# A float32 attention and two-layer expert chain: layers 1 and 3 as 2x2 block products with seven multiplications

## The chip, the core and the metric

The kernel runs on one core of a Trainium2 chip. Its five engines each work through a queue of their own in order: TensorE (PE, with its weight loads PEld), VectorE (DVE), ScalarE (ACT), GpSimd (POOL) and SyncE (SP, which issues most transfers). They wait for each other through semaphores. The metric is the device time of one execution in microseconds (us), lower is better; the median of three runs is given.

## The reference

A clustered attention gives 1536 tokens of 512 values, and four dense products follow:

```python
x = attention(q, k, v, centroids)            # (1536, 512)
h = max(max(x @ w1, x @ w2), x @ w3)         # layer 1: three weights 512 x 768
y = h @ w_out                                # layer 2: 768 x 512
g = max(y @ w_in, 0) ** 2                    # layer 3: 512 x 2048
out = g @ w_out2                             # layer 4: 2048 x 512
```

Weights come from HBM as 64-bit floats.

## The kernel before

Each float32 operand is held as a high and a low part in the fp32r type; a product of two operands is three matmuls (high x high, high x low, low x high). A matmul takes a 128 x 128 weight block and a chunk of 512 tokens, of which there are three, into one of eight PSUM banks. The attention part is ordered by a planner with costs and due times and is not touched, save that four constant tiles move to a pool of their own (`ac`) which ends with the attention. The text below speaks of what follows it.

Layer 1 takes its weights one at a time: 6 row blocks `fi` times 3 matrices `j`, each 512 columns wide in SBUF. `products` (L236 to L241) issues 36 matmuls per weight (4 k blocks x 3 parts x 3 chunks). The banks come in two sets `psu` of three. ACT copies the result of j = 0 to `hm` (L907), DVE takes the maximum for j = 1 and 2 (L909), and ACT and DVE split the maximum into `h` (L910, L911). Layer 2 does 4 x 54 matmuls in the same way, split into `yT` (L922, L923). Layer 3 has 16 row blocks `fi` of 36 matmuls; relu, square and split (L964 to L969) make `g`. Layer 4 (`mm_out`, L939) adds two `fi` at a time into 12 token tiles: six matmuls into a bank of their own, then DVE adds the bank to the sum `acc` in SBUF (L949). Its matmuls stand between those of layer 3.

A weight block of 512 columns is loaded as raw bits (`w_load`, L189) into one of three `wr` tiles and turned into float32 by six DVE instructions (`w_bits`, L208 to L214) and a POOL addition (L215); `w_parts` makes the high part on ACT (L227) and the low part on POOL (L228). Two weights (`EARLY`) are converted during the attention, so that the last stretch of it also holds first matmuls of layer 1. What belongs to the next weights is issued by `ahead` after the matmuls of this one; the program's order is written out by hand.

Of the kernel before, what the change touches and what calls it, by code (L numbers as in the profile page):

```python
# [2 lines left out]

# [80 lines left out]
BIG = float(2.0 ** 100)  # L84


@with_exitstack
def clustered_attention_moe(ctx, tc, qT, kT, vv, cen, w123, wo1, win, wo2, out):
    nc = tc.nc
# [79 lines left out]
    use = list(range(U2)) + [u_in(fi) for fi in range(NF)]
    plan = [[u] for u in use[EARLY:]] + [[]] * (EARLY + 1)  # L170
    for fi in range(NF):
        s = FIRST[fi] if fi < len(FIRST) else U2 + fi
        plan[s] = plan[s] + [u_out(fi)]
    seq = use[:EARLY] + sum(plan, [])
    assert sorted(seq) == list(range(len(units)))
# [42 lines left out]
    def w_parts(i):  # L218
        _, n = units[i]
        if i < EARLY:  # L220
            hl = wearly.tile([P, 2, 512], F32R, tag="whl", name=f"whl{i}")
        elif i >= U2 and (i - U2) % 4 >= 2:
            hl = wl.tile([P, 2, 512], F32R, tag="w2", bufs=6, name=f"w2_{i}")
        else:
            hl = wl.tile([P, 2, 512], F32R, tag="whl", bufs=3, name=f"whl{i}")
        t = wval.pop(i)
        act.copy(hl[:, 0, :n], t)  # L227
        pool.tensor_tensor(hl[:, 1, :n], t, f(hl[:, 0, :n]), op=ALU.subtract)  # L228
        wspl[i] = hl
# [652 lines left out]

    def blocks(u, *sb):

        yield ps2[u], [t[:, :1024].rearrange("p (a b) -> p a b", a=2) for t in sb]
        yield ps1[u], [t[:, 1024:] for t in sb]

    with ExitStack() as hctx:
        hp_ = hctx.enter_context(tc.tile_pool(name="hp_", bufs=1, reuse_waits="tile"))
        hsb = hp_.tile([P, FF1 // P, 2, NTOK], F32R, name="h")  # L890
        for fi in range(FF1 // P):
            hm = hp_.tile([P, NTOK], F32, tag="hm", bufs=2, name=f"hm{fi}")
            for j in range(3):
                w = next_w()
                u = (3 * fi + j) % 2
                pt = psu[u]
                if fi == 0 and j < EARLY:
                    products(pt, w, HP - 1, xT, HP - 1, False, True, (1,))
                    for k in range(HP):
                        products(pt, w, k, xT, k, k == 0, k == HP - 1, (2,))  # L900
                else:
                    for k in range(HP):
                        products(pt, w, k, xT, k, k == 0, k == HP - 1)
                ahead()
                for ps, (sb,) in blocks(u, hm):
                    if j == 0:
                        act.copy(sb, ps)  # L907
                    else:
                        dve.tensor_tensor(sb, ps, sb, op=ALU.max)  # L909
            act.copy(hsb[:, fi, 0, :], hm)  # L910
            dve.tensor_tensor(hsb[:, fi, 1, :], hm, f(hsb[:, fi, 0, :]), op=ALU.subtract)  # L911
        yT = xp.tile([P, DM // P, 2, NTOK], F32R, tag="xy", name="yT")
        for m in range(DM // P):
            pt = psu[m % 2]
            for kk in range(2):
                w = next_w()
                for k3 in range(3):
                    k = kk * 3 + k3
                    products(pt, w, k3, hsb, k, k == 0, k == FF1 // P - 1)
                ahead()  # L920
            for ps, (hi, lo) in blocks(m % 2, yT[:, m, 0, :], yT[:, m, 1, :]):
                act.copy(hi, ps)  # L922
                dve.tensor_tensor(lo, ps, f(hi), op=ALU.subtract)  # L923

    gp = ctx.enter_context(tc.tile_pool(name="gp", bufs=1, reuse_waits="tile"))
    NTT = NTOK // P
    GF = 2
    NG = FF2 // P // GF
    HALF = NTT // GF
    acc = [gp.tile([P, DM], F32, name=f"acc{t}") for t in range(NTT)]  # L930
    gs = {}

    def mm_out(gi, tk, n=slice(0, DM), pt=None):
        fs = range(gi * GF, gi * GF + GF)
        pt = pso[tk % 2] if pt is None else pt
        c = slice(tk * P, tk * P + P)
        for fi in fs:
            for a, wi in ((0, 0), (0, 1), (1, 0)):
                pe.matmul(pt[:, n], gs[fi][:, a, c], wspl[u_out(fi)][:, wi, n], start=fi == fs[0] and a + wi == 0,  # L939
                          stop=fi == fs[-1] and a == 1)  # L940
        return pt

    def out_add(gi, tk, pt, n=slice(0, DM)):
        if gi == 0 and tk < 2:
            act.copy(acc[tk], pt)
        elif gi == 0:
            dve.tensor_copy(acc[tk], pt)
        else:
            dve.tensor_tensor(acc[tk][:, n], pt[:, n], acc[tk][:, n], op=ALU.add)  # L949
        if gi == NG - 1:  # L950
            sp.dma_start(out[tk * P : tk * P + P, n], acc[tk][:, n])

    for fi in range(FF2 // P):
        w = next_w()
        pt = psu[fi % 2]
        for k in range(HP):
            products(pt, w, k, yT, k, k == 0, k == HP - 1)
        ahead()
        rt = gp.tile([P, NTOK], F32, tag="rt", bufs=1, name=f"rt{fi}")
        gt = gp.tile([P, 2, NTOK], F32R, tag="g", bufs=2 * GF, name=f"g{fi}")  # L960
        h0, h1 = slice(0, S), slice(S, 2 * S)
        todo = []
        for ps, (sb,) in blocks(fi % 2, rt):
            act.activation(sb, ps, AF.Relu)  # L964
        for h in (h0, h1):
            todo.append(lambda h=h, fi=fi: ((pool if fi >= 2 and h == h0 else dve).tensor_tensor(rt[:, h], rt[:, h], rt[:, h], op=ALU.mult),
                                     act.copy(gt[:, 0, h], rt[:, h])))  # L967
        for h in (h0, h1):
            todo.append(lambda h=h, fi=fi: (pool).tensor_tensor(gt[:, 1, h], rt[:, h], f(gt[:, 0, h]), op=ALU.subtract))  # L969
        gi = fi // GF - 1  # L970
        for i in range(HALF):
            if gi >= 0:
                tk = fi % GF * HALF + i
                out_add(gi, tk, mm_out(gi, tk))

            if todo and (fi != GF or i):
                todo.pop(0)()
        gs[fi] = gt
    for tk in range(NTT - 1):
        out_add(NG - 1, tk, mm_out(NG - 1, tk))  # L980

    for i in range(2):
        n = slice(i * DM // 2, (i + 1) * DM // 2)
        pt = ps1[i]
        out_add(NG - 1, NTT - 1, mm_out(NG - 1, NTT - 1, n, pt), n)
# [42 lines left out]
```

## Time and profile before

| | us |
|---|---|
| three runs | 717.44, 717.85, 717.99 (median 717.85) |
| profiled execution, first to last instruction (span) | 716.1 |
| median less that span | 1.75 |
| attention, with the first matmuls of layer 1 | 0 to 264.43 |
| rest of the two early weights (30 matmuls) | 264.43 to 271.23 |
| layer 1 | 271.23 to about 402 |
| layer 2 | about 402 to 451 |
| layers 3 and 4 | about 451 to 713.0 |
| last addition and store | 713.0 to 716.1 |

The page of the profile gives the busy time of each engine and a chain of work that ended last; a matmul's own time overlaps that of the next, so a busy PE is judged by how many matmuls a stretch holds.

### The profile page before, as it was taken

The page shows a single profiled execution, that of the slowest core. Times are in us where ns is not written, and L with a number is a line of the kernel's source. Part 1 is how long each engine was busy: PE and PEld are TensorE (multiplying, and loading weights), DVE is VectorE, ACT ScalarE, POOL GpSimd, SP SyncE. Part 2 cuts the span into 40 slices and gives each one's busy share as a digit, 9 for nine tenths or more (in the row PEclk, how much of TensorE's full clock was granted, in tenths as well). Part 3 has the DMA queues.
Part 4 walks back from the last instruction along what each step waited for, and adds up shares of the span by engine and source line. Part 5 has one row for each costly group of instructions (what it writes and reads, how often), then busy time and mean ns, then how long its engine had stood idle before and what let it go on. Part 6 is the DMA issues. An engine that isn't in the chain of part 4 may idle for free.

```text
span 716.1 us, 10433 instructions
## 1 busy us (share of the span) xinstructions
PE 701.3 (98%) x3663; PEld 597.1 (83%) x3663; DVE 588.4 (82%) x915; ACT 336.3 (47%) x670; POOL 449.0 (63%) x386
## 2 busy tenths in 40 slices
PE   7799999999999999999999999999999999999998
PEld 6689898999999878888888888888888888888886
DVE  6788988989989988998897677798888888886434
ACT  5789999999999841122212121333222222223210
POOL 5477797796867865553663233477776667777530
PEclk9999999999999999999999999999999999999999
DMA  8973834615432002221322032111111111210004
GB/s 215 240 179 91 203 89 130 154 43 136 106 109 89 1 30 88 89 88 59 118 74 67 25 101 84 63 59 60 59 59 59 59 59 64 89 54 1 1 0 177
DMA packets 21108, 62.21 MB, mean 87 GB/s; under 512 B 3168, under 2 KB 3936, under 8 KB 20608
## 3 DMA queue, kind: packets, MB, share of 16 engines
q1 hardware_dynamic: 20336, 59.98, 28.8%
q10 hardware_dynamic: 720, 1.57, 0.7%
q8 instruction: 29, 0.48, 0.3%
q14 instruction: 23, 0.19, 0.1%
HBM read 38.83 MB, written 3.15 MB: 59 GB/s over the span
## 4 chain that ended last, share of the span: by engine, by line
PE 88%; DVE 7%; ACT 2%; issue 2%; POOL 1%; DMA 0%; ACTq 0%; DVEq 0%; POOLq 0%
PE psd L240 29%; PE pss L939 18%; PE pss L240 15%; PE pss L572 6%; PE psd L533 4%; PE pss L592 4%; PE psd L535 4%; PE pss L593 4%; DVE at L583 2%; DVE nm L542 2%; PE pss L423 2%; ACT at L578 1%; ACT e L549 1%; PE pss L132 1%; PE pss L449 1%
## 5 line engine op out<-in xcount | busy, mean ns | idle before, releaser
L215 POOL TENSOR_TENSOR wt<-wt,ww 128x512 f32<-128x512 f32 (+1 forms) x56 | 78.4, 1409 | 115.3 <-DVE wt L214 115.3
L939 PE MATMUL pss<-w,g 128*128 128x512 f32 (+1 forms) x582 | 133.9, 388 | 0.0
L240 PE MATMUL psd<-xT,whl 128*128 128x512 f32 x432 | 131.3, 391 | 0.3 <-POOL whl L228 0.2
L939 PEld LDWEIGHTS pss<-w,g 128*128 128x128 f32 x582 | 107.7, 188 | 24.0 <-DVE acc L949 1.5
L240 PE MATMUL psd<-yT,whl 128*128 128x512 f32 x384 | 118.2, 389 | 0.0
L567 POOL TENSOR_SCALAR e<-e,nm 128x768 f32<-128x768 f32 x93 | 83.9, 920 | 50.5 <-DVE nm L557 32.7
L583 DVE TENSOR_TENSOR at<-pss,at 128x384 fp32r<-128x384 f32 x192 | 99.6, 548 | 17.7 <-ACT at L578 17.1
L949 DVE TENSOR_TENSOR acc<-pss,acc 128x512 f32<-128x512 f32 (+1 forms) x85 | 58.1, 684 | 54.1 <-PE pss L939 53.3
L240 PEld LDWEIGHTS psd<-xT,whl 128*128 128x128 f32 x432 | 80.7, 188 | 17.6 <-POOL whl L228 0.6
L542 DVE TENSOR_REDUCE nm<-psd 128x1 f32<-128x768 f32 x96 | 90.5, 948 | 4.8 <-PE psd L535 4.1
L572 PE MATMUL pss<-ident,e 128*128 128x128 f32 x576 | 90.5, 274 | 3.0 <-DVE at L583 2.0
L578 ACT CAST at<-pss 128x384 fp32r<-128x384 f32 x192 | 85.5, 478 | 9.5 <-PE pss L572 6.8
L549 ACT ACTIVATE e<-psd,nm 128x768 f32<-128x768 f32 x96 | 87.3, 910 | 3.9 <-DVE nm L542 3.8
L240 PEld LDWEIGHTS psd<-yT,whl 128*128 128x128 f32 x384 | 72.1, 188 | 15.0
L228 POOL TENSOR_TENSOR whl<-wt,whl 128x512 fp32r<-128x512 f32 (+1 forms) x40 | 60.5, 1514 | 36.4 <-ACT whl L227 36.4
L572 PEld LDWEIGHTS pss<-ident,e 128*128 128x128 f32 x576 | 71.5, 140 | 12.4 <-DVE at L583 4.0
L240 PE MATMUL pss<-xT,whl 128*128 128x512 f32 x216 | 80.5, 389 | 0.0
L240 PE MATMUL pss<-yT,whl 128*128 128x512 f32 x192 | 74.7, 389 | 0.0
L592 PE MATMUL pss<-at,vs 128*128 128x384 f32 x192 | 73.4, 382 | 0.5 <-ACT avt L605 0.5
L969 POOL TENSOR_TENSOR g<-rt,g 128x768 fp32r<-128x768 f32 x32 | 62.2, 1966 | 16.0 <-ACT g L967 16.0
L964 ACT ACTIVATE rt<-psd 128x1024 f32<-128x1024 f32 x16 | 16.5, 1030 | 117.7 <-PE psd L240 115.3
L593 PE MATMUL pss<-at,vs 128*128 128x384 f32 x192 | 65.4, 341 | 0.4 <-DVE at L583 0.4
(130 smaller groups left out, 1222.9 us busy)
## 6 DMA issues: line engine op xcount, KB each, us to landing
wr<-w SPq DMA_DIRECT2D x16, 512.0 KB, 3.3
wr<-wo SPq DMA_DIRECT2D x16, 512.0 KB, 3.3
wr<-win SPq DMA_DIRECT2D x16, 512.0 KB, 3.6
wr<-wo SPq DMA_DIRECT2D x8, 384.0 KB, 3.1
out<-acc SPq DMA_DIRECT2D x11, 256.0 KB, 2.0
tv<-vv SPq DMA_DIRECT2D x7, 384.0 KB, 5.0
stodd<-rl SPq DMA_DIRECT2D x12, 192.0 KB, 3.9
stodd<-rl SPq DMA_DIRECT2D x4, 576.0 KB, 7.6
```

What stands on the lines that cost most here:

```text
L215: lambda: pool.tensor_tensor(t, t, f(w), op=ALU.add),
L240: pe.matmul(pt[n], w[:, wi, c], x[:, k, xi, ch(n)], start=first and wi + xi == 0, stop=last and wi == 1)
L542: dve.tensor_reduce(nms[g][:, 0, i : i + 1], pss[s][:, :, :HS], axis=AX.XY, op=ALU.max, negate=True)
L549: act.activation(two(e), pss.pop(s)[:, :, :HS], AF.Exp, bias=nm[:, 0, i : i + 1], accum_out=nm[:, 1, i : i + 1])
L567: (pool if w == "P" else dve).tensor_scalar(e, e, r, 1.0, op0=ALU.mult, op1=ALU.mult)
L572: pe.transpose(pt[:, i * P : (i + 1) * P], et[3 * g + i][:, kt * P : (kt + 1) * P], ident)
L578: act.copy(a[:, 0, :], pts[g, kt][:, :HS])
L583: eng.tensor_tensor(a[:, 1, :], pts.pop((g, kt))[:, :HS], f(a[:, 0, :]), op=ALU.subtract)
L592: pe.matmul(avs[g][:, :HS], l, a[:, 0, :], start=kt == 0, stop=False)
L593: pe.matmul(avs[g][:, :HS], l, a[:, 1, :], start=False, stop=kt == NQ - 1)
L939: pe.matmul(pt[:, n], gs[fi][:, a, c], wspl[u_out(fi)][:, wi, n], start=fi == fs[0] and a + wi == 0, stop=fi == fs[-1] and a == 1)
L969: todo.append(lambda h=h, fi=fi: (pool).tensor_tensor(gt[:, 1, h], rt[:, h], f(gt[:, 0, h]), op=ALU.subtract))
```

## The change

Layer 1's weights are paired (two row blocks `fi` of one matrix `j`: nine pairs); the first three pairs (`PLAIN`) are multiplied as before, 72 matmuls a pair. For the other six, and for the eight pairs of layer 3, the product of a 2 x 2 block of weights (row blocks `fi` and `fi + 1`, two halves of k) with a 2 x 2 block of tokens (two halves of k, chunks 0 and 1) is made from seven block products of six matmuls (`P1` to `P7`) in place of eight, by sums of the operands. Chunk 2 is multiplied as before (`D` and `E`, 12 matmuls each). A pair takes 66 matmuls. Layers 2 and 4 keep their 216 and 582.

The sums of the weights (`sums_of`) are made for each pair; those of the tokens (`sums`, `x_sums`) once a layer, with high and low parts; one of them overwrites chunk 1. Within a pair the bank `b` carries `P1`, then `P6`, `P7` and `P4` are added to it; ACT copies it to another bank after `P1` (`R1`, which seeds bank `a` for `P2`) and to SBUF after `P6` and `P7` (`R2`, `R3`), and DVE adds bank `c` to those copies (`C22`, `C12`). In layer 4, of the middle groups, every second token tile's bank is seeded by ACT with the sum from SBUF before its matmuls and copied back by ACT after them, without an addition on DVE.

Weights are converted in pairs of 512 columns (`convert`): two loads into two raw tiles, then on ACT two `Abs` and two scalings, on DVE or POOL a clip over 1024 columns, on DVE a shift over 1024 and two ORs over 512, on DVE or POOL an addition, on ACT the high and on DVE or POOL the low part. DVE's six instructions for 512 columns and the `wt` and `ww` tiles are gone.

Everything after the attention becomes operations with costs, tiles and keys, and `arrange` puts them into one order: it takes the operation that can start first, by its own cost numbers, chooses DVE or POOL where both may do it, lets only one of DVE and POOL use their SBUF port at a time (`port`), and assigns PSUM banks (8), 4 KB slots (30, and the two early ones) and 2 KB slots (10). Their pool `big` follows the freed attention pools.

```diff
-    wq = wl = ctx.enter_context(tc.tile_pool(name="wq", bufs=1, reuse_waits="tile"))
-    ...                                        # next_w, ahead, blocks, mm_out, out_add and the three loops
+    actx = ctx.enter_context(ExitStack())
+    ac = actx.enter_context(tc.tile_pool(name="ac", bufs=1))
+    ident = ac.tile([P, P], F32, name="ident")
...
+    big = ctx.enter_context(tc.tile_pool(name="big", bufs=1, reuse_waits="tile"))
+    NB4, K2, KR = 30, 10, 2
+    kinds = {
+        "ps": ("bank", nb), "raw": ("raw", KR), "w": ("k4", 8), "w2": ("k4", 4), "h": ("k4", NF1 * NCH), "S": ("k4", 6),
+        "acc": ("k4", 6), "g": ("k4", 9), "f": ("k2", K2), "a": ("k4", 2), "r": ("k4", 1), "t": ("k4", 1),
+    }
...
+    def convert(u0, u1, due, kind="w", due_lo=0):
...
+            op(("ld", u), due - 14 + 2 * i, {"sp": (2.6 * n / 512, 2.0)}, ...
+            op(("ab", u), due - 9, {A_: act_t(n) + 0.05}, lambda e, raw=raw, c=c: e.activation(T[a][:, c], f(T[raw][:, :n, 1]), AF.Abs),
+            op(("rd", u), due - 7.5, {A_: act_t(n) + 0.05}, lambda e, raw=raw, c=c: e.mul(u32(T[r][:, c]), T[raw][:, :n, 0], float(2.0**-29)),
+            op(("or", u), due - 7, {D_: tt_d(n)}, ...
+        op(("cl", u0), due - 8, {G_: 0.1 + 2 * n / 660, D_: ts_d(2 * n)}, ...
+        op(("sh", u0), due - 7.5, {D_: ts_d(2 * n)}, ...
+        op(("ad", u0), due - 5, {G_: tt_g(2 * n), D_: tt_d(2 * n)}, lambda e: e.tensor_tensor(u32(va()), u32(va()), u32(vr()), op=ALU.add),
+        split(a, 2 * n, hi, lo, kind, due - 1, [("ad", u0)])
...
+    def seven(tag, q, u0, key, X, S, xready, sready):
...
+        prod("P1", 0, b, w, [(k, X(k, 0)) for k in range(2)], xready(0, 0, 1))
+        op(n("R1"), key - 4, {A_: 0.6}, lambda e: seed(T[a], T[b]), [n("P1")], [("ps", a)], [b])
+        prod("D", 1.4, d, w, [(k, X(k, 2)) for k in range(4)], xready(2, 0, 1, 2, 3))
+        prod("P6", 4.1, b, tw, [(4 + k, S(2, k)) for k in range(2)], [n("R1"), n("P1"), *sready(2)], False, False, s_(2))
+        op(n("R2"), key - 4, {A_: 0.6}, copy(2, b), [n("P6")], [("f", R(2))], [b])
+        prod("P2", 5.5, a, w, [(2 + k, X(2 + k, 0)) for k in range(2)], [n("R1"), *xready(0, 2, 3)], False, False)
+        prod("P7", 6.9, b, tw, [(2 + k, S(3, k)) for k in range(2)], [n("R2"), n("P6"), *sready(3)], False, False, s_(3))
+        op(n("R3"), key - 4, {A_: 0.6}, copy(3, b), [n("P7")], [("f", R(3))], [b])
+        prod("P5", 8.2, c, tw, [(k, S(1, k)) for k in range(2)], sready(1), sx=s_(1))
+        prod("P4", 9.6, b, tw, [(6 + k, X(2 + k, 1)) for k in range(2)], [n("R3"), n("P7"), *xready(1, 2, 3)], False, False)
+        prod("E", 11, e_, w, [(4 + k, X(k, 2)) for k in range(4)], xready(2, 0, 1, 2, 3))
+        op(n("C22"), key + 5, {D_: 0.69}, add(3, c), [n("P5"), n("R3")], (), [R(3), c], False)
+        prod("P3", 13.6, c, w, [(6 + k, S(4, k)) for k in range(2)], [n("C22"), n("P5"), *sready(4)], False, False, s_(4))
+        op(n("C12"), key + 12, {D_: 0.69}, add(2, c), [n("P3"), n("R2")], (), [R(2), c], False)
...
+    SUM = [(1, "22", "21", "22", ALU.add), (3, "21", "11", "21", ALU.subtract), (2, "11", "22", "11", ALU.subtract), (4, "12", "12", "11", ALU.subtract)]
...
+                seeded = 0 < g < NG - 1 and i % 2 == 1
+                if seeded:
+                    op(("sd", g, tk), at - 1.5, {A_: 0.63}, lambda e, bank=bank, tk=tk: seed(T[bank], acc(tk)), ...
...
+    order = arrange(ops, {"bank": nb, "k4": K4, "k2": K2, "raw": KR}, kinds, {"pe": 0.0, "act": -3.0, "dve": -4.0, "pool": 0.0, "sp": -8.0, "port": 0.0},
+                    {("we", i): ("w", NB4 + i) for i in range(EARLY)})
+    for n, e, got, _ in order:
+        for tl, where in got.items():
+            make(tl, *where)
+        fns[n](eng[e])
```

## Rows read from the trace of the kernel before

**Rows 1.** The page's parts 1 and 2: busy time, and slices of the span.

```profile
PE 701.3 (98%) x3663; PEld 597.1 (83%) x3663; DVE 588.4 (82%) x915; ACT 336.3 (47%) x670; POOL 449.0 (63%) x386
...
PEclk9999999999999999999999999999999999999999
```

**Rows 2.** Stretches: length; PE, PEld, DVE, ACT, POOL busy (instructions); clock, DMA, GB/s.

```profile
0.00:264.43 264.43, 252.74 (x1684) 227.18 (x1684) 230.61 (x436) 230.83 (x522) 197.13 (x229) 0.99 0.48 122
...
264.43:271.23 6.80, 6.80 (x30) 5.64 (x31) 6.58 (x8) 2.85 (x4) 4.25 (x4) 1.00 0.27 90
271.23:402.00 130.77, 130.77 (x579) 108.28 (x578) 112.96 (x151) 26.65 (x35) 65.23 (x42) 1.00 0.24 80
402.00:451.00 49.00, 49.00 (x218) 40.58 (x217) 38.26 (x57) 10.38 (x16) 18.38 (x16) 1.00 0.22 70
...
451.00:713.00 262.00, 261.96 (x1158) 215.39 (x1156) 199.55 (x265) 65.63 (x94) 164.03 (x98) 1.00 0.16 57
713.00:716.10 3.10, 0.00 (x0) 0.00 (x0) 0.42 (x1) 0.00 (x0) 0.00 (x0) 1.00 0.47 169
```

**Rows 3.** Groups by line and form, matmuls of layers 1, 3 and 4: busy, mean ns.

```profile
L939 PE MATMUL pss<-w,g 128*128 128x512 f32 x570 | 132.4, 390 | 0.0
L240 PE MATMUL psd<-xT,whl 128*128 128x512 f32 x432 | 131.3, 391 | 0.3 <-POOL whl L228 0.2 <-POOL xT L626 0.2
L240 PE MATMUL psd<-yT,whl 128*128 128x512 f32 x384 | 118.2, 389 | 0.0
...
L240 PE MATMUL pss<-xT,whl 128*128 128x512 f32 x216 | 80.5, 389 | 0.0
L240 PE MATMUL pss<-yT,whl 128*128 128x512 f32 x192 | 74.7, 389 | 0.0
```

**Rows 4.** The same view, conversion of a weight block of 512 columns.

```profile
L215 POOL TENSOR_TENSOR wt<-wt,ww 128x512 f32<-128x512 f32 x48 | 70.0, 1470 | 96.6 <-DVE wt L214 96.6
...
L208 DVE TENSOR_SCALAR wa<-wr 128x512 uint32<-128x512 uint32 x48 | 54.1, 1149 | 0.0
L228 POOL TENSOR_TENSOR whl<-wt,whl 128x512 fp32r<-128x512 f32 x32 | 51.3, 1602 | 21.8 <-ACT whl L227 21.8
...
L211 DVE SCALAR_TENSOR_TENSOR ww<-wr,wa 128x512 uint32<-128x512 uint32 x48 | 39.0, 834 | 1.9 <-DVE wa L210 0.5
...
L227 ACT CAST whl<-wt 128x512 fp32r<-128x512 f32 x32 | 19.8, 620 | 54.4 <-POOL wt L215 54.4
```

**Rows 5.** The same view, what ACT and DVE do with results of layer 1.

```profile
L911 DVE TENSOR_TENSOR h<-hm,h 128x1536 fp32r<-128x1536 f32 x6 | 10.6, 1759 | 9.3 <-ACT h L910 9.3
...
L910 ACT CAST h<-hm 128x1536 fp32r<-128x1536 f32 x6 | 8.9, 1482 | 37.7 <-DVE hm L909 37.7
...
L909 DVE TENSOR_TENSOR hm<-pss,hm 128x512 f32<-128x512 f32 x12 | 8.2, 680 | 0.0
...
L907 ACT COPY hm<-pss 128x512 f32<-128x512 f32 x6 | 3.6, 592 | 0.4 <-PE pss L240 0.4
```

**Rows 6.** Timeline from the attention's end into layer 1: start, length, what.

```profile
256.38 0.49 PE L572 MATMUL pss<-ident,e 128*128 128x128 f32 x3
...
257.89 0.42 DVE L208 TENSOR_SCALAR wa<-wr 128x512 uint32<-128x512 uint32 x1
...
259.13 0.47 ACT L605 COPY avt<-pss 64x384 f32<-64x384 f32 x1
...
261.89 2.49 POOL L626 TENSOR_TENSOR xT<-xr,xT 128x384 fp32r<-128x384 f32 x2
...
264.34 1.47 POOL L215 TENSOR_TENSOR wt<-wt,ww 128x512 f32<-128x512 f32 x1
...
264.43 0.73 PE L240 MATMUL psd<-xT,whl 128*128 128x512 f32 x2 [0.15 <-POOL xT L626]
264.70 1.40 DVE L210 TENSOR_SCALAR wa<-wa 128x512 uint32<-128x512 uint32 x1
```

**Rows 7.** The page's part 6, loads of layer 1's weights: KB, us to landing.

```profile
wr<-w SPq DMA_DIRECT2D x16, 512.0 KB, 3.3
```

More of the change, by code (lines that the diff above doesn't have):

```diff
@@ L1 @@
 from contextlib import ExitStack
-from itertools import zip_longest
 import concourse.bass as bass
@@ L84, with arrange, opening @@
 BIG = float(2.0 ** 100)
+def arrange(ops, slots, kinds, free, held):
+    users = {}
+    for n, (_, _, _, opens, uses) in ops.items():
+        for t in {*(t for _, t in opens), *uses}:
+            users[t] = users.get(t, 0) + 1
+    homes = {h: [-99.0] * k for h, k in slots.items()}
+    taken = {h: [None] * k for h, k in slots.items()}
+    lives = dict.fromkeys(kinds, 0)
+    place, kind_of, until = {}, {}, {}
+    for tl, (kind, i) in held.items():
+        home = kinds[kind][0]
+        taken[home][i] = tl
+        place[tl], kind_of[tl], until[tl] = (home, i), kind, -99.0
+        lives[kind] += 1
+    wait, follow = {}, {}
+    for n, o in ops.items():
+        wait[n] = len(set(o[2]))
+        for a in set(o[2]):
+            follow.setdefault(a, []).append(n)
+    num = {n: i for i, n in enumerate(ops)}
+    start = {n: {e: -99.0 for e in o[1]} for n, o in ops.items()}
+    ready = {n for n in ops if not wait[n]}
+    order = []
+    def opening(n):
+        t, want = -99.0, {}
+        for kind, _ in ops[n][3]:
+            want.setdefault(kind, 0)
+            want[kind] += 1
+        for kind, k in want.items():
+            home, most = kinds[kind]
+            can = sorted(u for u, x in zip(homes[home], taken[home]) if x is None)
+            if lives[kind] + k > most or len(can) < k:
+                return None
+            t = max(t, can[k - 1])
+        return t
+    while ready:
+        best = {}
+        for n in ready:
+            key, engines, _, _, _ = ops[n]
+            o = opening(n)
+            if o is None:
+                continue
+            c = min((max(free[e], start[n][e], o, free["port"] if p else o) + d, e) for e, (d, _, p) in engines.items())
+            e = c[1]
+            t = round(c[0] - engines[e][0], 3)
+            if e not in best or (t, key, num[n]) < best[e]:
+                best[e] = (t, key, num[n], n)
+        if not best:
+            raise RuntimeError(f"stuck: {sorted(ready, key=lambda n: ops[n][0])[:12]} {lives}")
+        e, (t, _, _, n) = min(best.items(), key=lambda x: x[1][:3])
+        _, engines, _, opens, uses = ops[n]
+        d, lat, port = engines[e]
+        ready.remove(n)
+        free[e] = t + d
+        if port:
+            free["port"] = free[e]
+        end = t + d + lat
+        got = {}
+        for kind, tl in opens:
+            home = kinds[kind][0]
+            i = min((u, i) for i, (u, x) in enumerate(zip(homes[home], taken[home])) if x is None)[1]
+            taken[home][i] = tl
+            place[tl] = home, i
+            kind_of[tl] = kind
+            until[tl] = -99.0
+            lives[kind] += 1
+            got[tl] = kind, home, i
+        for tl in {*(t for _, t in opens), *uses}:
+            users[tl] -= 1
+            if tl not in place:
+                raise KeyError(f"{n} uses {tl} before it is there")
+            until[tl] = max(until[tl], end)
+            if not users[tl]:
+                home, i = place[tl]
+                taken[home][i] = None
+                homes[home][i] = until[tl]
+                lives[kind_of[tl]] -= 1
+        for m in follow.get(n, ()):
+            wait[m] -= 1
+            for x in start[m]:
+                start[m][x] = max(start[m][x], free[e] if x == e and e != "sp" else end)
+            if not wait[m]:
+                ready.add(m)
+        order.append((n, e, got, t))
+    if len(order) < len(ops):
+        raise RuntimeError("ops that wait for ever")
+    return order
@@ L167, in u_out @@
         return U2 + fi // 2 * 4 + 2 + fi % 2
[L169 to L175, printed above, removed]
     wraw, wval, wspl = {}, {}, {}
@@ L883, in blocks @@
[L883 to L900, printed above, removed]
-                else:
[L902 to L985, printed above, removed]
+    NCH = NTOK // 512
+    NF1, NF = FF1 // P, FF2 // P
+    U2 = len(units) - 2 * NF
+    NTT = NTOK // P
+    nb = len(pss_slots := [ps2[0][:, 0, :], ps2[0][:, 1, :], ps1[0], ps2[1][:, 0, :], ps2[1][:, 1, :], ps1[1], ps1[2], ps1[3]])
+    big = ctx.enter_context(tc.tile_pool(name="big", bufs=1, reuse_waits="tile"))
@@ new lines, in plain @@
+    def plain(tag, q, u0, key, X):
+        got = []
+        w = (("wh", u0), ("wl", u0))
+        for fo in range(2):
+            for c in range(NCH):
+                bank = ("ps", tag, q, fo, c)
+                op((tag, q, fo, c), key + 8.1 * fo + 2.7 * c, {"pe": 12 * MM},
+                   lambda _, bank=bank, fo=fo, c=c: mms(bank, w, [(4 * fo + k, X(k, c)) for k in range(HP)], True, True),
+                   [w[1]], [("ps", bank)], [*w, bank])
+                got.append((fo, c, bank, (tag, q, fo, c), False))
+        return got
@@ new lines, in clustered_attention_moe, with seed, early @@
+    whole = set()
+    def seed(bank, src):
+        assert id(bank) in whole
+        act.copy(bank, src)
+    PLAIN = 3
+    hm = {}
+    t = 0.0
+    for i in range(2):
+        banks = [("ps", "m", i, c) for c in range(NCH)]
+        for c in range(NCH):
+            op(("m", "open", i, c), -100 + 3 * i + c, {"pe": (0.0, 0.0)}, lambda _: None, [("m", "open", i, c - 1)] if c else [("m", "open", i - 1, 2)] if i else [],
+               [("ps", banks[c])], [banks[c]])
+    def early(i, c, ks, first):
+        for k in ks:
+            for wi, xi in ((0, 0), (0, 1), (1, 0)):
+                pe.matmul(T["ps", "m", i, c], wspl[i][:, wi, k * P : k * P + P], xT[:, k, xi, CH[c]], start=first and k == 0 and wi + xi == 0,
+                          stop=k == HP - 1 and wi == 1)
+        whole.add(id(T["ps", "m", i, c]))
@@ new lines, in clustered_attention_moe, with out_mm @@
+    NG = NF // 2
+    CORD = (1, 2, 0)
+    tks = [4 * c + i for c in CORD for i in range(4)]
+    def out_mm(bank, g, tk, n, first):
+        c, i = divmod(tk, 4)
+        u = U2 + 4 * g + 2
+        for j in range(2):
+            for a_, wt in ((0, "wh"), (0, "wl"), (1, "wh")):
+                pe.matmul(T[bank][:, : n.stop - n.start], T["g", 2 * g + j, c][:, a_, i * P : i * P + P], T[wt, u][:, 512 * j + n.start : 512 * j + n.stop],
+                          start=first and j + a_ == 0 and wt == "wh", stop=j == 1 and a_ == 1, skip_group_check=True)
```

330 lines of the change are left out of this document (301 added, 29 removed).

## Prediction

> **What bounds the kernel now.** I read the page first: PE is busy 98% of the span, at the full clock in every slice [rows 1]. Then the stretches: from 264.43 to 713.0 us PE's busy time equals the length of each stretch to 0.04 us, while no other engine fills one [rows 2]. Then the groups by line, to see whether that busy time is work: a matmul is listed at 0.389 us [rows 3], but layer 1's stretch holds 16 weight blocks of 36 matmuls in 130.77 us [rows 2], so one starts every 0.227 us. Over the four layers, 6.80 + 130.77 + 49.00 + 261.96 = 448.53 us [rows 2] hold 30 + 576 + 216 + 576 + 576 = 1974 matmuls (the twelve half-width ones at the end counted as six): 0.2272 us each. That is the price I use. The last 3.1 us are an addition and a store. So behind the attention the time is the number of matmuls, and other engines matter only when they make PE wait. The timeline at the hand-over [rows 6] shows when the attention lets go of its engines and tiles.
>
> The sum is made against the profiled span of 716.1 us and the 1.75 us around it, which together are the median of 717.85.
>
> **Matmuls taken away.** Each of 6 + 8 pairs takes 66 in place of 72: 84 fewer, 84 x 0.2272 = 19.1 us. All of them lie on the path. They keep shape and operand type, and each has its own weight load, as before; both orders that the trace has, banks in turn in layers 1 to 3 and six in a row into one bank in layer 4, run at the same distance, so six in a row into `b` cost no more. With PE dense throughout: 717.85 - 19.1 = 698.8.
>
> **Conversion of a pair.** What it adds to ACT, estimated from rows: four passes over 512 columns at 0.62 and two high parts over 1024 at about 1.0 (1.48 for 1536) [rows 4, 5]. Three bank copies at 0.59 make 6.3 us a pair in layer 1, with on average 2.0 for results 8.3 of the 66 x 0.2272 = 15.0 us that PE gives it. DVE: shift 0.7, two ORs 1.7, weight sums 1.5, two bank additions 1.4, up to six maxima 4.1: 9.4. POOL: three 1024-column passes at twice 1.5, and a clip that no row shows (between DVE's 0.7 and a POOL pass of 2.9; I take 1.7, as it has one input): 10.7. In layers 3 and 4 a pair has 138 matmuls, 31.4 us, and ACT has 23 (conversions 8.0, bank copies 1.8, six seeds and their copies back 7.2, relu 2.4, high parts 3.7). No engine is full, so conversions cost nothing under the matmuls; without that cover each would cost its chain, some 8 us.
>
> No row shows ACT's Abs, its scaling of integers, or ACT writing a bank. Nearest: 0.62 from SBUF and 0.59 from PSUM [rows 4, 5]; ends 0.4 and 1.0. ACT's load stays under PE's at either end in layer 1 (at 1.0, 8.3 grows by about 2.7); in layers 3 and 4 it would reach about 31 of 31.4. I take 0.6.
>
> DVE and POOL hold each other up: a DVE pass that takes 0.42 us alone took 1.40 beside a POOL pass of 1.47, and ended as that ended [rows 6]; over the run it means 1.15 [rows 4]. The maxima, with one operand from PSUM, show none of it: 0.68 [rows 5]. The Trainium skill (GPSIMD Engine Reference, Key points) says the contention is with DVE instructions in a two-port mode or with two SBUF inputs, so `C22`, `C12` and the maxima should stay free and only shift, OR, addition and low parts wait. By that rule the sum stays as it is so long as a pair's loads and conversion take under 15.0 us; by the row a 1024-column POOL pass can hold DVE's queue for 2.9 us, maxima behind it included. That is the slow rival below.
>
> **The hand-over.** The 30 early matmuls give the first converted pair until 271.23 [rows 2]. The raw tiles may lie where `ident` was, last read at 256.87 [rows 6]; then the first load lands at 260.2 and the second, behind it, by 263.5 at the latest (3.3 each [rows 7]). What follows the second: Abs 0.62, clip 0.7, shift 0.7, ORs 1.7, addition 1.2, high part 1.0, low part 1.2, and 0.5 for hops: 271.1, just in time. If POOL takes the addition or the low part (2.9 for 1.2), 1.6 or 3.3 late. PE then waits: bounds 0 and 3.3, I take 0.7, since DVE is free from 258.3 on and ACT from 259.6 [rows 6].
>
> **The links of bank `b`.** `R2` stands between `P6` and `P7`, `R3` between `P7` and `P4`. A link lasts 0.16 (0.389 less 0.227, the tail of a matmul), the copy's 0.59 and two hops of 0.05 (POOL's last xT ends at 264.38, PE starts at 264.43 [rows 6]): 0.85 us. Six matmuls of other banks stand between, 1.36 us, so 0.5 is left. Behind an instruction just begun on ACT, of up to 1.05, a link ends up to 0.55 late; PE and all behind it wait. 14 links (six pairs of layer 1, the first of layer 3) lie between 0 and 7.7 us. ACT is busy 8.3 of 15.0, so about half meet something, mostly a pass of 0.6: I take 0.15 each, 2.1. `R1` has 12 matmuls of cover, and in the other seven pairs layer 4's matmuls stand between too: 0.
>
> **Token sums.** The first wanted by layer 3 needs, after layer 2's last matmul, a copy 0.59, two sums and a difference at 0.68, a high part 0.62, a low part 0.68: 4.0 with hops, and `P1`, `D`, `P2` and `E` cover 36 x 0.2272 = 8.2. Layer 1's have two plain pairs (32.7 us) as cover. Bounds 0 and 4, I take 0.5.
>
> **ACT's seeds in layer 4.** DVE loses 36 additions of 0.69 which mostly waited for PE, so this saves nothing on the path; the seed needs a free bank and 0.6 us before its tile, with other matmuls in between: 0.
>
> The sum: 717.85 - 19.1 + 0.7 + 2.1 + 0.5 = 702.0. Bounds 698.8 and 717.85 - 19.1 + 3.3 + 7.7 + 4 = 713.8.
>
> **Rivals.**
> - *PE dense.* The planned order swaps in other products whenever a link is late. For it: 8 banks against 5 per pair. Against: queues are in order, and plan and chip differ. 698.8 (up to 700).
> - *Links and hand-over near their upper bounds*, with ACT's queue behind something late: 706 to 714.
> - *No change.* The seven products come with gaps of 1.36 us per pair (14 x 1.36 = 19): each pair's plain order would have been as fast. 717.9.
> - *Slower: weights arrive late.* There are two raw tiles where three were, and both are held until the ORs have read them. That cycle is 3.3 to 6.6 of loading, 0.62, 1.7, 0.7, 1.7 and 0.5 of hops: 8.5 to 11.8 us, under 15.0. If each of the three DVE passes is held by a POOL pass (up to 2.9), it reaches 17 to 20. It decides at 16.4 (15.0 + 1.36), where the waits eat the gain; at 17 the 14 pairs lose 28: 717.85 - 19.1 + 28 = 727. For it: the 1.40 beside 1.47. Against: the planner lets one of the two use the port at a time, and DVE's load falls.
> - *The clock falls.* PE pauses at bank `b` in each pair. The traced attention has 11.7 us without PE in short pauses, at a clock of 0.99 [rows 2], which speaks against it. At 1.2 GHz in place of 2.4 a matmul costs up to 0.2272 more; a tenth of the 1890 left makes 43 us: 742. The Trainium skill (TensorE: Matmul & The Clock Gate, A second HAM failure mode: psum-queue depth-cycling) tells of a kernel whose PE idled briefly between groups as it cycled through banks, and so went back and forth between the two clocks; here the attention does the like and keeps it.
>
> **How the numbers follow.** Forecast (700 to 706): 0.40. Dense: 0.27. Upper bounds: 0.16. No change: 0.04. Late weights: 0.10. Clock: 0.03. A change of 0.2% is about what a measurement of this kernel can tell from none. Faster 0.40 + 0.27 + 0.16 = 0.83, same 0.04, slower 0.13. The likeliest is 702.0. The range runs from 697.8 (dense, less 1.0 for the store and addition at the end and the rounding of the stretches) to 712: it leaves out the late weights, the clock, no change and the very end of the upper bounds, some 0.18.
>
> **What would show it.** Right: 84 matmuls fewer, 0.227 us apart; PE's idle time between 264 and the end at 1 to 6 us, named by ACT's `R2` and `R3` and by the first pair's low part; DVE below its 82%, ACT well above 47%; clock 1.00. Wrong: idle time at weight tiles (`wl`, `tl`) in every pair, DVE passes of 2 to 3 us beside POOL's, loads waiting for raw tiles; a wait of several us at 271 for a tile that the attention still holds; or a clock row below 9.

## The result: 708.1 us, half of what 84 matmuls are worth

The changed kernel took 708.13 us (median of four runs, 707.49 to 708.23), the kernel before beside it 717.92 (717.44 to 718.51): a ratio of 0.9864, 95% interval 0.985 to 0.9878. The profiled execution has a span of 706.4 us. That lies in the predicted range, but 6.1 us above the likeliest 702.0 and in the band of the rival "links and hand-over near their upper bounds". Of the 19.1 us that the missing matmuls are worth, 9.8 arrived.

The page after, parts 1 and 2, to be read against [rows 1]:

```profile
PE 686.6 (97%) x3579; PEld 582.8 (83%) x3579; DVE 553.2 (78%) x890; ACT 505.5 (72%) x975; POOL 206.9 (29%) x240
...
POOL 5567797987858760000100000000000000000000
PEclk9899999999999999999999999999999999999999
```

PE has 3579 instructions, 84 fewer. ACT rose from 47 to 72%, DVE fell from 82 to 78%, and POOL, which I had given 10.7 us of every pair, does almost nothing behind the attention. The clock's digit is 9, that is 90% or more, but for one slice inside the attention.

From the page's parts 5 and 6, groups that answer to [rows 3], [rows 4] and [rows 7]:

```profile
L1308 PE MATMUL pss<-w_wh,g_g 128*128 128x512 f32 x240 | 82.0, 390 | 0.0
...
L1013 ACT ACTIVATE a_a<-raw_raw 128x512 f32<-128x512 f32 (+1 forms) x56 | 36.4, 651 | 3.0 <-DMA raw_raw<-wo 1.2
...
L1054 PE MATMUL pss<-xT,w_wh 128*128 128x512 f32 x120 | 37.1, 390 | 0.8 <-ACT w_wh L1030 0.8
...
raw_raw<-w SPq DMA_DIRECT2D x16, 512.0 KB, 4.0
```

From the groups by line of DVE behind the attention (the addition is listed as `CUSTOM_DVE_ANT_0`):

```profile
L1032 DVE TENSOR_TENSOR w_wl<-a_a,w_wh 128x1024 fp32r<-128x1024 f32 (+1 forms) x28 | 33.9, 1210 | 6.7 <-ACT w_wh L1030 6.0
L1024 DVE CUSTOM_DVE_ANT_0 a_a<-a_a,r_r 128x2048 uint16<-128x2048 uint16 (+1 forms) x28 | 33.2, 1186 | 2.4
```

A matmul is what it was, and all 28 low parts and all 28 additions of the conversions are DVE's, at 1.2 us each.

The stretches, as in [rows 2] (length; PE, PEld, DVE, ACT, POOL busy; clock, DMA, GB/s):

```profile
264.50:272.00 7.50, 7.50 (x34) 5.94 (x32) 4.13 (x6) 4.04 (x8) 0.39 (x1) 1.00 0.16 51
272.00:310.00 38.00, 36.63 (x161) 29.97 (x161) 35.09 (x53) 19.18 (x31) 0.00 (x0) 1.00 0.21 74
310.00:442.00 132.00, 131.83 (x581) 108.50 (x580) 106.53 (x151) 68.16 (x112) 5.09 (x5) 1.00 0.21 73
442.00:455.00 13.00, 13.00 (x60) 10.74 (x59) 9.02 (x14) 10.08 (x18) 0.00 (x0) 1.00 0.19 74
455.00:475.00 20.00, 17.80 (x75) 13.52 (x74) 17.94 (x26) 15.83 (x27) 0.75 (x1) 1.00 0.17 58
475.00:500.00 25.00, 23.68 (x104) 18.89 (x103) 16.99 (x23) 18.11 (x31) 0.73 (x1) 1.00 0.23 80
500.00:703.00 203.00, 202.15 (x896) 166.79 (x894) 136.71 (x191) 138.05 (x228) 4.00 (x5) 1.00 0.18 65
```

PE's busy time no longer equals the length of every stretch. It is short by 1.4 us behind the hand-over, by 2.2 and 1.3 at the start of layers 3 and 4, by 1.0 in all the rest. The waits of PE in those stretches (line waited for: us in all, times, longest):

```profile
PE psd L1054 <- ACT f_R_y L1075: 1.4, 2, 0.7
PE psd L1054 <- ACT f_v L1360: 1.3, 2, 1.0
PE psd L1054 <- ACT psd L1113: 0.9, 2, 0.4
PE psd L1054 <- DVE f_R_y L1087: 0.9, 1, 0.9
PE pss L1054 <- ACT w_wh L1030: 0.8, 1, 0.8
PE pss L1054 <- DVE w_wl L1032: 0.5, 1, 0.5
PE psd L1054 <- DVE f_hm L1214: 0.2, 1, 0.2
```

These 6.0 us are idle time; a matmul's own time of 0.39 overlaps the next, so the start of the late matmul slips by 0.16 more than its idle time shows, and the one after it by a further 0.11 (two matmuls after a wait take 0.73, elsewhere 0.62). Summed over the starts of matmuls, PE loses 9.1 us behind the attention; before it lost 0.7.

One thing stands out: of the rows of layers 1 and 3, every wait that isn't for weights names `psd`. `psd` are the four banks that the attention holds as two tiles of two banks.

### The profile page after: what moved, and what is told of

Its sections match the earlier page's. It is cut to its first block, busy times and chain, and to the rows that moved or that the text cites. A ratio compares the mean times of both kernels' runs of the same rounds, so it can differ in the third digit from the quotient of the medians.

```text
span 706.4 us, 10292 instructions
## 1 busy us (share of the span) xinstructions
PE 686.6 (97%) x3579; PEld 582.8 (83%) x3579; DVE 553.2 (78%) x890; ACT 505.5 (72%) x975; POOL 206.9 (29%) x240
## 4 chain that ended last, share of the span: by engine, by line
PE 86%; DVE 6%; ACT 6%; issue 2%; DMA 0%; DVEq 0%; ACTq 0%
PE psd L1054 21%; PE pss L1054 17%; PE pss L1308 11%; PE pss L661 7%; PE psd L1308 7%; PE psd L622 5%; PE psd L624 4%; PE pss L681 4%; PE pss L682 4%; PE pss L512 2%; DVE at L672 1%; DVE nm L631 1%; PE psd L329 1%; ACT e L638 1%; PE pss L228 1%
## 5 line engine op out<-in xcount | busy, mean ns | idle before, releaser
L1308 PE MATMUL pss<-w_wh,g_g 128*128 128x512 f32 x240 | 82.0, 390 | 0.0
L1308 PEld LDWEIGHTS pss<-w_wh,g_g 128*128 128x128 f32 x240 | 45.0, 188 | 9.7 <-DVE g_g L1364 0.3
L1030 ACT CAST w_wh<-a_a 128x1024 fp32r<-128x1024 f32 (+1 forms) x28 | 28.6, 1022 | 31.5 <-DVE a_a L1024 31.3
L1308 PE MATMUL psd<-w_wh,g_g 128*128 128x512 f32 (+1 forms) x148 | 49.4, 383 | 0.0
L1308 PE MATMUL pss<-w_wl,g_g 128*128 128x512 f32 x120 | 46.7, 389 | 0.0
L1032 DVE TENSOR_TENSOR w_wl<-a_a,w_wh 128x1024 fp32r<-128x1024 f32 (+1 forms) x28 | 33.9, 1210 | 6.7 <-ACT w_wh L1030 6.0
L1013 ACT ACTIVATE a_a<-raw_raw 128x512 f32<-128x512 f32 (+1 forms) x56 | 36.4, 651 | 3.0 <-DMA raw_raw<-wo 1.2
L681 PEld LDWEIGHTS pss<-at,vs 128*128 128x128 f32 x192 | 36.4, 189 | 2.0 <-ACT avt L694 1.5
L1054 PE MATMUL pss<-xT,w_wh 128*128 128x512 f32 x120 | 37.1, 390 | 0.8 <-ACT w_wh L1030 0.8
L682 PEld LDWEIGHTS pss<-at,vs 128*128 128x128 f32 x192 | 36.6, 191 | 1.4 <-DVE at L672 1.3
L1054 PE MATMUL psd<-xT,w_wh 128*128 128x512 f32 x120 | 37.0, 389 | 0.0
```

The costliest lines, as they stand in the source:

```text
L681: pe.matmul(avs[g][:, :HS], l, a[:, 0, :], start=kt == 0, stop=False)
L682: pe.matmul(avs[g][:, :HS], l, a[:, 1, :], start=False, stop=kt == NQ - 1)
L1013: op(("ab", u), due - 9, {A_: act_t(n) + 0.05}, lambda e, raw=raw, c=c: e.activation(T[a][:, c], f(T[raw][:, :n, 1]), AF.Abs), [("ld", u)] ...
L1054: pe.matmul(T[bank], T[w[wi]][:, wb * P : wb * P + P], x(xi), start=first and n == 0, stop=last and n == 3 * len(ks) - 1, skip_group_check ...
L1308: pe.matmul(T[bank][:, : n.stop - n.start], T["g", 2 * g + j, c][:, a_, i * P : i * P + P], T[wt, u][:, 512 * j + n.start : 512 * j + n.stop],
```

## Experiments

Each run stands beside runs of the kernel before (medians 717.5, 717.7 and 718.6), and the ratios are to those. The attention's end differs by up to 2.0 us between these traces (the first matmul of `early`, what is left of the two early weights, stands between 263.46 and 265.49 us), so small differences are read from the stretch behind it: from that matmul to the end of the span the changed kernel takes 441.25 us. The kernel before takes 716.1 - 264.43 = 451.7.

**All layers plain.** `PLAIN = 99`; layer 3 calls `plain`, and `sums_of` and `sums` fall away.

> All layers in plain order (72 matmuls a pair, 3663 in all, no token or weight sums), with the new list schedule, the 1024-column conversion and the seeded banks kept. Theory A (part of the loss is the schedule's own: the attention ends 0.7 us later and the hand-over costs 1.9 us in any version): 717.9 + 0.7 + 1.9 = 720.5, up to 721.5 if the first pair of layer 3 waits for the last y tile. Rival B (the whole loss of 9.4 us belongs to the seven products): 717.9.

720.75 us, ratio 1.0041 (1.0028 to 1.0054). PE waits 1.3 us for the first converted pair, as in the changed kernel (0.8 for `w_wh`, 0.5 for `w_wl`), and 0.8 around layers 2 and 3. This is theory A's 720.5. So the hand-over belongs to the schedule; the longer waits behind it come only with the order that the seven products make.

**Layer 1 alone, layer 3 alone.** As above, in one layer each.

> Seven products in the six pairs of layer 1 alone, layer 3 plain: 36 matmuls fewer, 8.2 us. Theory A (schedule 2.6, layer 1's links 0.5): 717.9 - 8.2 + 3.1 = 712.8, up to 713.8. Rival B (the loss is spread evenly over the 14 pairs, 0.67 each): 717.9 - 8.2 + 4.0 = 713.7, with idle time of PE in every pair and none at the hand-over that an all-plain version lacks.

712.0 us (0.9907 to 0.9935), near theory A's 712.8. Behind the hand-over PE waits once, 0.2 us, in six pairs, where rival B has idle time in every pair: layer 1's products arrive nearly whole.

> Seven products in the eight pairs of layer 3 alone, layer 1 plain: 48 matmuls fewer, 10.9 us. Theory A (schedule 2.6, layer 3's waits 6.4, of which 3.2 in its first pair): 717.9 - 10.9 + 9.0 = 716.0. Rival B (spread evenly): 717.9 - 10.9 + 5.4 = 712.4. Rival C (the first pair of layer 3 waits only because layer 1's sums have made the conversions late): its 3.2 vanish, 712.8.

715.48 us (0.996 to 0.998): layer 3's 48 matmuls, 10.9 us, bring 2.0, or 5.3 against the plain run with its hand-over. The sum is near theory A's, but not its parts: of the 3.2 in the first pair one wait for `f_R_y` is left (0.7), which is nearer to rival C, and later pairs wait 3.0 us for `acc_acc` and `f_v`, on `psd` each time. That fits the banks better than one pair.

**Single banks.** Same order of instructions on every engine; only the tiles that hold the banks differ.

```diff
-    ps2 = [pp.tile([P, 2, 512], F32, name=f"psd{i}") for i in range(2)]
...
+    pd_ = ExitStack()
+    pd = pd_.enter_context(tc.tile_pool(name="pd", bufs=1, space=PSUM))
+    ps2 = [pd.tile([P, 2, 512], F32, name=f"psd{i}") for i in range(2)]
...
+            if i in (0, 1, 3, 4) and tl[1] != "m" and not singles:
...
+                pd_.close()
+                p1 = ctx.enter_context(tc.tile_pool(name="p1", bufs=1, space=PSUM, reuse_waits="tile"))
+                for k in (0, 1, 3, 4):
+                    pss_slots[k] = p1.tile([P, 512], F32, name=f"psn{k}")
```

> The order of all instructions as in the changed kernel; the four banks that belong to two tiles of two banks are four tiles of one bank once the early units are done. Theory A (ACT and DVE instructions on such a tile wait for matmuls on its other bank, and this causes the waits of PE at 375, 480, 489, 566 and 629 us: 0.4 + 0.6 + 1.3 + 0.7 + 0.7): those go, 708.1 - 3.7 = 704.4. Rival B (ACT runs behind the planner's durations there): waits stay, 708.1.

701.89 us, ratio 0.9785 (0.9768 to 0.9801): 6.2 less than the changed kernel, and 5.5 less from the first `early` matmul to the end (435.77). That is more than theory A's 3.7: besides the five waits that it names, the one for `C22` at 462 us went (1.0 + 0.1 by the starts of matmuls) and a few of under 0.2. All waits of PE behind the attention that are left:

```profile
PE psn L1063 <- ACT f_R_y L1084: 1.4, 2, 0.7
PE pss L1063 <- ACT w_wh L1039: 0.8, 1, 0.8
PE pss L1063 <- DVE w_wl L1041: 0.5, 1, 0.5
```

What went is seen best at `C22` in the first pair of layer 3. Its bank `c` and the bank `b` of `P4` are the two halves of `psd0`. Timeline of the changed kernel:

```profile
459.97 0.73 PE L1054 MATMUL psd<-yT,w_th 128*128 128x512 f32 x2 [0.68 <-ACT f_R_y L1075]
...
461.23 0.40 PE L1054 MATMUL psd<-yT,w_tl 128*128 128x512 f32 x1
461.74 0.69 DVE L1087 TENSOR_TENSOR f_R_y<-psd,f_R_y 128x512 f32<-128x512 f32 x1 [1.10 <-PE psd L1054]
...
462.48 0.73 PE L1054 MATMUL psd<-S_S_y,w_wh 128*128 128x512 f32 x2 [0.85 <-DVE f_R_y L1087]
```

and with single banks:

```profile
458.27 0.73 PE L1063 MATMUL psn<-yT,w_th 128*128 128x512 f32 x2 [0.68 <-ACT f_R_y L1084]
...
458.86 0.68 DVE L1096 TENSOR_TENSOR f_R_y<-psn,f_R_y 128x512 f32<-128x512 f32 x1
...
459.53 0.40 PE L1063 MATMUL psn<-yT,w_tl 128*128 128x512 f32 x1
...
459.77 0.63 PE L1063 MATMUL psn<-S_S_y,w_wh 128*128 128x512 f32 x2
```

`C22` needs `P5` and `R3`, both done. With two banks in a tile it waits for the end of `P4`, and `P3` behind it waits in turn; with one it runs beside `P4`. The other direction is a seed by ACT into one half of `psd0`, and `P6` of a later pair, which goes on in bank `b`, the other half. First the changed kernel, then single banks:

```profile
565.41 0.59 ACT L1113 COPY psd<-acc_acc 128x512 f32<-128x512 f32 x1
...
566.05 0.50 PE L1054 MATMUL psd<-S_S_y,w_th 128*128 128x512 f32 x1 [0.43 <-ACT psd L1113]
```

```profile
559.92 0.59 ACT L1122 COPY psn<-acc_acc 128x512 f32<-128x512 f32 x1
...
560.46 0.62 PE L1063 MATMUL psn<-S_S_y,w_th 128*128 128x512 f32 x2
```

With single banks PE starts 0.05 us before the copy ends. These were semaphores set for a tile, not something the banks need. The option `reuse_waits` of the new pool is not the cause: the four one-bank tiles `pss`, which stay in the old pool, show no such wait in the changed kernel. The Trainium skill (PSUM — Partial Sum Buffer, PSUM bank collisions raise a hardware error) asks for guards by bank and quadrant, with bank the simple version; the run agrees, as with guards by bank 5.5 us came back.

**Raw tiles elsewhere.** Fourteen 4 KB slots and two 2 KB ones are made first, so that `r0` and `r1` no longer lie on `ident`.

```diff
+    for i in range(14):
+        make(("S", "first", i), "S", "k4", i)
+    for i in range(2):
+        make(("f", "first", i), "f", "k2", i)
```

> The single-bank kernel (701.9) with the two raw tiles on memory that the attention has long left, not on ident; the order of all instructions is unchanged, so the first loads go some 20 us earlier. Theory A (the 1.9 us at the hand-over come from ACT's order: the second Abs stands behind hm copies that wait for PE): nothing, 701.9. Rival B (the loads' wait for the last reader of ident costs them): 700.0.

701.89 us (0.9765 to 0.9796), 435.75 us behind the attention: nothing, the same three waits, though the first loads are issued at 203 us in place of 257 (the expectation had some 20 us). The tile that the attention still holds, which the prediction had set as the end of the hand-over's chain, costs nothing.

**Hand-over, order.** On top of that:

```diff
-            op(("ld", u), due - 14 + 2 * i, {"sp": (2.6 * n / 512, 2.0)},
+            op(("ld", u), due - 14 + 2 * i, {"sp": (1.0, 1.5) if u0 == 2 else (2.6 * n / 512, 2.0)},
...
-                op(("xa", k, r), t - 14 + 5 * k + 0.3 * j, {D_: 0.69, G_: 1.5},
+                op(("xa", k, r), t - 8 + 5 * k + 0.3 * j, {D_: 0.69, G_: 1.5},
...
-            sums("x", k, t - 12 + 5 * k, tiles, ready, xT, done)
+            sums("x", k, t - 6 + 5 * k, tiles, ready, xT, done)
```

> As the kernel with the raw tiles elsewhere, and the planner's price for the first two loads is cut from 2.6 + 2.0 to 1.0 + 1.5 us, so that it puts the second Abs ahead of the hm copies; layer 1's token sums are due 6 us later, so that they do not push ahead of the next weights. Theory A (ACT's order): the waits at 272 and 273 us go, 701.9 - 1.9 = 700.0. Rival B (the conversion's chain itself is too long): they stay, 701.9.

701.49 us (0.9758 to 0.9803). Both waits are gone, but 435.31 us behind the attention is 0.46 less, not 1.9. New waits took the place of the old:

```profile
PE psn L1063 <- ACT f_R_x L1084: 0.7, 1, 0.7
PE psd L1138 <- POOL xT L717: 0.2, 1, 0.2
```

The first is a bare link in layer 1's first pair of seven products, at 317 us (it is gone again below, where the sums are due 4 us later in place of 6); the second is POOL's last two passes over `xT`, which took 2.75 us beside DVE's conversion in place of 1.99, while the clip took 1.29 in place of 0.69. Theory A holds for the cause, but its 700.0 was missed: the price was paid again elsewhere.

ACT's order in the changed kernel, for comparison with [rows 6]:

```profile
261.73 0.67 ACT L1013 ACTIVATE a_a<-raw_raw 128x512 f32<-128x512 f32 x1 [0.94 <-DMA raw_raw<-w]
...
265.99 1.07 ACT L1141 COPY f_hm<-psd 128x512 f32<-128x512 f32 x2 [3.02 <-PE psd L1129]
266.95 0.67 ACT L1013 ACTIVATE a_a<-raw_raw 128x512 f32<-128x512 f32 x1
...
267.65 0.69 DVE L1021 TENSOR_SCALAR a_a<-a_a 128x1024 f32<-128x1024 f32 x1 [6.70 <-ACT a_a L1013]
...
271.81 1.05 ACT L1030 CAST w_wh<-a_a 128x1024 fp32r<-128x1024 f32 x1 [1.83 <-DVE a_a L1024]
```

The second `Abs` stands behind two copies of `early` banks, for which ACT waited 3.02 us while DVE waited 6.70 for the clip's input. Both raw tiles had landed at least 4 us before (261.7 and 262.95).

**First pair of layer 3: `E` and `P5` held back.**

```diff
-        prod("P5", 8.2, c, tw, [(k, S(1, k)) for k in range(2)], sready(1), sx=s_(1))
+        prod("P5", 8.2, c, tw, [(k, S(1, k)) for k in range(2)], [*sready(1), *([n("P7")] if (tag, q) == ("y", 0) else [])], sx=s_(1))
...
-        prod("E", 11, e_, w, [(4 + k, X(k, 2)) for k in range(4)], xready(2, 0, 1, 2, 3))
+        prod("E", 11, e_, w, [(4 + k, X(k, 2)) for k in range(4)], [*xready(2, 0, 1, 2, 3), *([n("P6")] if (tag, q) == ("y", 0) else [])])
```

> The single-bank kernel (701.9); in the first pair of layer 3, E must come behind P6 and P5 behind P7, so that they lie under R2 and R3. Theory A (the same 36 matmuls cannot cover both the token sums and the links): the 1.9 us of waits at P7 and P4 go, but P6 then waits for its token sum, 701.9 to 703.4. Rival B (the sums are ready by then, and only the order was unlucky): 700.0.

704.82 us (0.9798 to 0.9832); 436.92 behind the attention, 1.15 more than with single banks alone, which is theory A's 703. The profiled execution took 703.19; where the other three lost up to 2.3 us more, no trace shows. The 1.4 us for `f_R_y` are gone, and PE waits for token sums in their place:

```profile
PE psn L1063 <- DVE S_S_y L1179: 1.3, 1, 1.3
...
PE psn L1063 <- ACT S_S_y L1177: 0.8, 1, 0.8
```

**Token sums sooner**, with `E` and `P5` still held back:

```diff
-                    op(("y", m, k, c), t + 2.04 * k3 + 0.68 * c,
+                    op(("y", m, k, c), t + (2.04 * c + 0.68 * k3 if m == 3 and kk else 2.04 * k3 + 0.68 * c),
```

> As the kernel with E and P5 held back, and the last three blocks of layer 2's last tile go token chunk by token chunk (three blocks of chunk 0, then of 1, then of 2), so that chunk 0 is complete 4.1 us and chunk 1 some 2.0 us before the layer's end. Theory A (the token sums are what the cover is needed for): both waits go, 701.9 - 1.9 = 700.0. Rival B (something else holds P6, as the y tiles' high and low parts): 701.9 to 703.4.

701.02 us (0.9748 to 0.9778), 434.59 behind the attention, 1.2 less than with single banks alone. ACT's copies of chunks 0 and 1 of the last tile start at 440.9 and 443.0, with `E` and `P5` merely held back at 443.4 and 444.6. Neither links nor sums show a wait; a new one of 0.5 stands at `P3`, for `C22`.

**No seeds**, on single banks: `seeded = False`.

> The single-bank kernel (701.9) without seeded banks in layer 4: all additions on DVE. Theory A (the seeds are worth nothing on the path, and ACT's load is not what makes PE wait): 701.9, ACT some 44 us less busy, DVE some 24 more. Rival B (DVE at 78% needs the relief): later weights and sums, 703 to 706.

702.74 us (0.977 to 0.9796), and 435.70 behind the attention against 435.77. ACT is 38.5 us less busy, DVE 20.8 more, the waits are the same three. Theory A, on single banks.

**POOL converts**, on single banks: `D_` is taken out of the engines for clip, addition and low parts.

> The single-bank kernel (701.9) with clip, addition and low parts of every conversion on POOL, as the prediction had assumed, where the planner gives nearly all to DVE. Theory A (a pair's loads and conversion then last longer than its 15 us of PE, in layers 1 and 2 above all: three passes of POOL at about 2.9 us each and a clip, and DVE's own passes held beside them): weights late in most pairs, 717 to 740. Rival B (POOL has the room, 71% idle, and the clip is cheap): 701.9.

732.65 us, ratio 1.02 (1.0185 to 1.0214): 30.8 slower than with DVE by the medians, 29.2 behind the attention (464.94 against 435.77). PE waits for weights, longest:

```profile
PE psn L1317 <- ACT w_wh L1039: 3.6, 1, 3.6
PE pss L1063 <- ACT w_wh L1039: 2.7, 1, 2.7
```

A POOL pass over 1024 columns took 2.38 us, its clip 1.13, where DVE did them in 1.21 and 0.67. Three such passes and a clip are 8.3 us of a pair's 15.0, so POOL is not full: the chain of a pair grew longer. Which of its steps is late in which pair this run does not take apart. Some 7 of the 29.2 us are matmuls at a lower clock (last section), and in the 232 us from 495 on, in layers 3 and 4, next to nothing is lost:

```profile
495.00:727.00 232.00, 231.87 (x1029) 192.06 (x1027) 123.29 (x176) 168.81 (x283) 99.22 (x49) 1.00 0.20 70
```

DVE's passes grew longer beside POOL's: its ORs rose from 0.668 to 0.783 and its shift from 0.674 to 0.825, while the maxima with one operand in PSUM stayed at 0.688 (0.687). The Trainium skill (GPSIMD Engine Reference, Key points) puts contention on DVE instructions in a two-port mode or with two SBUF inputs; this run agrees for the ORs, which have two SBUF inputs, and for the maxima; that the shift, with one, is in a two-port mode no row shows.

**Both orders mended**, on single banks: the raw tiles, the load price, layer 1's sums due 4 us later (`t - 10`), and the edits of the two runs on layer 3. (In the expectation, "436.0" is a slip: 435.8 - 0.5 - 1.2 = 434.1.)

> The two mended orders together on single banks: the second Abs ahead of the hm copies, with layer 1's token sums due 4 us later, and layer 3's token sums sooner with E and P5 held back. Theory A (the two places are independent): 436.0 us from the first early matmul to the end in place of the single-bank kernel's 435.8, less 0.5 and less 1.2: 434.1, and 700.2 us in all. Rival B (the list schedule gives the gain back elsewhere, as layer 1's first pair already did): 434.6 or more, 701 to 702.

699.01 us, ratio 0.9733 (0.9719 to 0.9746): 19.5 less than the 718.55 of the kernel before beside it, and 9.1 less than the changed kernel. 433.26 us behind the attention, 0.8 less than theory A's 434.1, as the new link wait at 317 us is gone. The waits that are left:

```profile
PE pss L1317 <- DVE w_wl L1041: 0.6, 1, 0.6
PE psd L1138 <- POOL xT L717: 0.2, 1, 0.2
```

Against the 451.7 of the kernel before these are 18.4 us less, and by the starts of matmuls 0.6 more is lost than there: together the 19.1 that 84 matmuls are worth.

## Why the prediction was right in range and wrong in size

*84 matmuls, 19.1 us.* Right: 3579 instructions at the same distance, and with the waits mended the kernel gains 19.5 by the medians, 18.4 behind the attention.

*Hand-over, 0.7.* It cost 1.9 (1.00 + 0.11 + 0.70 + 0.11 by the starts of matmuls). The chain was right in kind, its cause not. I had the load behind `ident` and POOL's slow passes as what could make it late; the load's place costs nothing, and DVE did the passes. ACT's queue stood behind copies that wait for PE, an order that the planner made because it priced two loads at 2.6 us each in a row, the second landing 4.6 after its start. I had costed the conversion's own chain and not what ACT has queued between its two halves.

*Links of bank `b`, 2.1.* The sum is near what was found (1.9), for another reason. I spread 0.15 over 14 links; the six pairs of layer 1 lost nothing to links in this order (on single banks no wait is left there). All of it comes from two links of layer 3's first pair, each fully exposed: 0.84 + 0.11, where I had computed 0.85 for a bare link. That the sums agree is luck.

*Token sums, 0.5.* No wait names them, but they are why those two links lie bare. I gave `P1`, `D`, `P2` and `E` to the sums as cover, and six matmuls of other banks to every link as cover; in that pair they are the same matmuls. Held back for the links, they are missed at the sums; with the sums' inputs 1.6 and 2.5 us sooner as well, both are covered.

*Eight independent banks: the step that failed.* I took the banks as eight that don't hold each other up. Four of them are two tiles, and an instruction on one half waits for the other half's latest. So a maximum of layer 1 and relu, `C22` and seeds of layer 3 and 4 held up PE where I had put 0, and that cost 5.5 us. With 1.9 and 1.9 it makes 9.3 us behind the attention. The kernel before lost 0.7 there as well, so 8.6 of it is new. That 9.3 is also what the medians lack of 19.1 is chance: the other 0.7 is an attention that ended later in the changed kernel's trace, at 265.11 in place of 264.43.

That 708.1 lies in the range, then, is luck in part: it falls into the band of the rival with links and hand-over near their upper bounds, but these took 1.9 of 7.7 and 1.9 of 3.3. It is luck too that single banks give 701.9, the forecast's 702.0. And of the 6.0 us of idle time, at the edge of the 1 to 6 that were to show the forecast right, only 1.4 are named by `R2` and `R3` and 0.5 by the first pair's low part.

*Seeds and conversions, 0.* Right on single banks; in the changed kernel two seeds cost 0.7 each through the shared tile. ACT's new operations were as I took them (`Abs` 0.65, scaling 0.65, a copy into a bank 0.59). POOL's share was wrong: the planner left it idle, and forced, it costs 29.2. So weights can come late, and the planner's choice of DVE is what kept that off. The slow rival's account of it is not borne out: it let POOL hold three DVE passes by up to 2.9 us each, in all 14 pairs. On average the ORs lost 0.12 and the shift 0.15; POOL's own passes took twice DVE's time; and layers 3 and 4 lost next to nothing behind 495 us. That its 727 was near is luck.

## What to carry to other kernels

Before you count banks, count tiles: in this kernel a tile that spans two banks made each half wait for the other, though the work on them was independent. Give each matmul to one wait as cover, never to two. And where a planner orders queues, its wrong price for one load shows up as another engine's order; mend the price, then look where the gain goes, since here three quarters of one came back as new waits.

## What the runs showed of the hardware

Two loads of 512 KB issued 0.4 us apart, at 258.07 and 258.45, landed 3.6 and 4.5 us after (one alone takes the 3.3 of [rows 7]). So the second came 1.2 us behind the first, and they don't follow one another at 3.3 each, as I had them. The first matmul after a wait is followed by the next 0.11 us later than in a row.

And the clock. In the run with `E` and `P5` held back it stayed at 1.00 from 448 to 456 us, with waits of up to 1.3 us. With POOL converting, PE idled 2.7 us for `w_wh`, and after that the granted clock was 0.50, the lower of the two levels of 1.2 and 2.4 GHz, until 281.4:

```profile
275.00:281.40 6.40, 5.16 (x11) 3.63 (x12) 4.92 (x4) 3.43 (x6) 3.83 (x2) 0.50 0.00 0
281.40:284.00 2.60, 2.60 (x13) 2.15 (x12) 2.12 (x4) 0.00 (x0) 0.00 (x0) 1.00 0.01 3
```

There matmuls started 0.43 us apart, and at 0.227 again after it. Three more stretches of that run, of 7 to 8 us, show 0.76, 0.76 and 0.63 on average, each where PE waited 1.6 us or more for weights. The rival "the clock falls" thus exists in this kernel, but no wait of the changed kernel behind the attention, the longest of 1.0 us, brought it about.

The prediction says that the attention keeps the clock, and reads the nines of [rows 1] as full speed. Both are not quite so: a nine is 90% or more, and in the kernel before one stretch of the attention, 28 to 40 us with PE busy for 10.39 of the 12.00, has a granted clock of 0.86 on average.
